# Finer TensorE steps, an earlier x load and new scheduling parameters in a two-part attention kernel

## The chip, the cores and the metric

The kernel runs on one core of one Trainium2 chip. The metric is device microseconds (us) of that core. Executions of one kernel differ here by several tenths of a per cent (11 runs of the kernel before took 1116.76 to 1122.92 us beside experiments 1 to 4), which is as large as some of the effects below. Where the text speaks of a time it is the median of several executions; where it speaks of a place in time, it is one profiled execution.

Names in the profile: PE is TensorE's matmuls and PEld its weight loads, DVE is VectorE, ACT is ScalarE, POOL is GpSimd, SP is SyncE (here it issues DMAs), and a trailing q is an engine's queue. "L970" is line 970 of the kernel's source. The change moves lines, so one group has another number before and after:

| work | before | after |
|---|---|---|
| exponentials | L970 | L1002 |
| scores | L941 | L973 |
| P times V | L1075 | L1109 |
| projections | L655 | L688 |
| output matmuls | L1162, L1210 | L1197, L1244 |

## The reference

Two attentions over different inputs, joined on the last axis. Both have 2048 rows, D = 1024, and 32 heads of 32.

```python
def _A_ref(x, wqkv, wo):                         # full softmax attention
    qkv = (x @ wqkv).reshape(B, S, 3, H, Dh)...  # q, k, v
    scores = einsum('bhqd,bhkd->bhqk', q, k) * Dh ** (-0.5)
    o = einsum('bhqk,bhkd->bhqd', softmax(scores), v)
    return o... @ wo

def _B_ref(x, wq, wk, wv, wo, beta):             # 4 segments of 512 rows, causal, with a memory
    for s in range(4):
        a_dot = softmax(qs @ ks^T * scale + mask) @ vs
        a_mem = (phi(qs) @ M) / (phi(qs) @ z + 1e-06)
        o = g * a_mem + (1 - g) * a_dot          # g = sigmoid(beta), one per head
        M, z = M + phi(ks)^T @ vs, z + sum(phi(ks))
    return o... @ wo

return concatenate([A, B], axis=-1)              # (1, 2048, 2048), bf16
```

## The kernel before

While it is built, the kernel runs a small scheduler of its own in Python. Processes (generators) ask for instructions with `do(engine, function, reads, writes, cost, priority)`. They wait for events, or acquire banks from pools. The scheduler has a clock and a table of costs, and each time an engine is free it takes the ready request with the lowest priority number. What comes out is a fixed order of instructions for every engine, with waits on semaphores in it. So a priority or a pool decides at build time what stands in front of what, and a misjudged cost shows up in a trace as an engine that waits.

```python
    def dispatch(self, eng, t):                       # [... cut ...]
        for rq in self.q[eng]:
            ready = ...                               # when everything it reads or overwrites is done
            p = rq.prio() if callable(rq.prio) else rq.prio
            if ready <= self.now + 1e-9:
                if best is None or (p, rq.seq) < best[0]:
                    best = ((p, rq.seq), rq)
        if best is None:
            if eng == "PE" and self.fill:
                rq = self.fill(soon)                  # nothing useful is ready: perhaps a filler
```

Scores have priority 0. A batch of scores is 8 matmuls (4 heads, 2 key tiles, 256 queries) into two pairs of PSUM banks. There are three such pairs. Each pair is then read by one exponential of 128x1024 on ScalarE, 1184 of them in all, and is free again when the exponential is done.

```python
            yield do("PE", lambda e: f(e, mms), r=keys, w=w, cost=N256, prio=0, mode=ROW)      # scores
        ...
            yield do("ACT", lambda e: e.activation(ap, self.ps[:, pr[0]:pr[1] + 1, :], ACTF.Exp, scale=sc),
                     r=[("ps", bk) for bk in pr], w=keys, cost=0.9035, prio=0)
            Q.give(self.pairs, [pr])
```

Everything else on TensorE accumulates in the two remaining "side" banks. A projection or output job is 8 steps of 4 matmuls, each 512 wide. A P-times-V unit takes a side bank, waits for exponentials one after the other, and keeps the bank until its last.

```python
    def job(self, due, mm, keys, out, okey, wkeys, ...):
        bank, = yield acq(self.side, 1, due)
        for i in range(last + 1):
            yield do("PE", lambda e, i=i: mm(e, i, bank), ..., cost=N512 * n / 512, prio=...)

    def pv_unit(self, u, steps, half):                # [... cut ...]
        OB, = yield acq(self.side, 1, -1000)
        for si, (k, parts) in enumerate(steps):
            yield ("ev", ("ex", u, k))                # the k-th exponentials of this unit
            ...
                yield do("PE", f, ..., cost=N256 * w / 256, prio=self.pvprio, mode=COL)   # 4 V matmuls, then 4 with ones
```

The filler gives TensorE work where it has little. If TensorE was under 65% busy in the scheduler's last 3.4 us, it adds matmuls of zeros to a bank in which an accumulation is under way (`self.under`):

```python
        if sum(c for _, c in Q.recent) > self.par["fil"] * 3.4:     # fil = 0.65
            return None
        bank = None
        for b in (OB, SB):
            if b in self.under:
                bank = b
        if bank is None:
            return None
        ...                                            # 4 matmuls of zeros, start=False, stop=False
```

The first x chunk (512 rows) is loaded in four pieces (XS 0 to 3) and transposed on TensorE. The other chunks come by DMA transposes that are held back until all four pieces have landed:

```python
                yield do("SP", lambda e, q0=q0, src=src: e.dma_start(self.xA[:, :, q0:q0 + 2 * P], src, transpose=True),
                         r=[("XS", 3), ("XS", 2), ("XS", 1), ("XS", 0)] if c == 1 and t == 0 else [], ...)
            self.Q.fire(("xA", c))
```

A flag is computed (were the softmax sums in range?), every engine reads it, and in the good case each engine branches over a fallback.

## Time and profile before

| | before |
|---|---|
| time, median of 4 runs (us) | 1119.68 (1118.54 to 1120.42) |
| span of the profiled run (us) | 1117.4 |
| ScalarE busy | 98% |
| TensorE busy | 94% |
| first exponential starts / ends (us) | 10.38 / 11.40 |
| last exponential ends (us), and from there to the end | 1103.64, 13.75 |

First the head of the page of the kernel before (busy us, share of the span, instructions), then from its table of groups the exponentials and the main scores (busy us, mean ns of one, then the idle time in front of them and what ended it):

```profile
span 1117.4 us, 50583 instructions
...
PE 1045.8 (94%) x23493; PEld 512.1 (46%) x23493; DVE 726.3 (65%) x1467; ACT 1091.2 (98%) x1191; POOL 134.8 (12%) x287
...
L970 ACT ACTIVATE PT<-ps 128x1024 bf16<-128x1024 f32 x1164 | 1068.4, 1202 | 2.6 <-PE ps L941 2.4
...
L941 PE MATMUL ps<-QA,KA 32*128 32x256 bf16 x4096 | 204.1, 273 | 34.3 <-ACT PT L970 25.0
```

Two things are to be read here. ScalarE is the limit: 1164 of the exponentials take 1068.4 us, 0.918 us each. And 1202 ns for one with 0.918 us of busy time means that each starts before the one ahead of it has ended. TensorE is 94% busy too, but its score groups wait for the exponentials (25.0 us), while the exponentials waited only 2.4 us for scores.

The chain of waits of the kernel before says the same in time order (start us, length us, what, how many). Long unbroken runs of exponentials carry most of the span:

```profile
48.88 1.07 issue
50.27 8.36 ACT PT L970 x9
58.70 74.26 ACT PT L970 x81
...
467.18 261.38 ACT PT L970 x285
728.57 373.24 ACT PT L970 x407
...
1104.25 0.87 PE ps L1075 x32
1105.12 2.59 PE ps L1162 x48
1108.36 4.16 PE ps L1162 x74
1112.54 0.58 ACT outsb L1168
```

373.24 us for 407 exponentials is 0.917 us each. The piece called "issue" is a stretch in which TensorE stood still although the profile shows nothing that it waited for. The last four lines are the tail: after the last exponential (1103.64) TensorE still has P times V and output matmuls to do.

The wait list of ScalarE, kernel before (us in total, times, longest):

```profile
ACT WoB L970 <- PE ps L941: 7.5, 2, 6.6
...
ACT OTA L970 <- PE ps L941: 2.6, 1, 2.6
...
ACT PT L970 <- PE ps L941: 2.4, 5, 1.0
```

6.6 us is the wait for the first scores. The 2.6 us is one wait near 21 us. The timeline of the kernel before shows where it comes from (start us, length us, engine, line, operation, count, idle time before and its releaser):

```profile
8.34 4.25 SPq L620 DMA_TRANSPOSE xA<-in_A_x_dram  x2
...
13.24 5.61 ACT L970 ACTIVATE WoB<-ps 128x1024 bf16<-128x1024 f32 x6 [0.93 <-PE ps L941]
...
16.70 4.35 PE L655 MATMUL ps<-xA,WA 128*32 128x512 bf16 x52
...
20.99 0.40 PE L941 MATMUL ps<-QA,KA 32*128 32x256 bf16 x8
...
21.43 5.61 ACT L970 ACTIVATE OTA<-ps 128x1024 bf16<-128x1024 f32 x6 [2.58 <-PE ps L941]
```

The transposes of the second x chunk are issued from 8.34 us on, when the fourth piece of the first chunk has landed, and their own data land at 13.0 and 15.9 us. The K projection of that chunk starts at 16.70, the scores follow at 20.99, and ScalarE, done at 18.85, waits until 21.43. The stretch view of the kernel before gives, for each stretch, length, busy time of PE, PEld, DVE, ACT and POOL, then the granted TensorE clock (PEclk), DMA share and GB/s:

```profile
12.70:16.10 3.40, 0.89 (x24) 0.27 (x16) 0.42 (x1) 2.85 (x4) 0.00 (x0) 1.00 1.24 197
16.10:19.50 3.40, 3.35 (x36) 1.22 (x40) 0.00 (x0) 2.75 (x3) 0.00 (x0) 0.50 1.62 204
```

After a stretch in which TensorE was 26% busy (0.89 of 3.40) comes one at half the clock, in which a 512-wide step took 0.427 us in place of 0.2155. In the traces of the whole programs here, the half-clock stretches that end before the work does last 3.413 us, or two or three times that, and within a trace they begin on one grid of 3.413 us. The kernel before has two of them, at 16.1 and at 285.7 us, each of 3.413 us; their starts are 269.65 us apart, 79 times 3.413. The first is part of the 2.6 us wait: the eight steps of that K projection took 3.11 us in place of 8 x 0.2155 = 1.72, so an estimate of 1.4 us of the wait is the clock's.

**Counting on ends.** Starts of exponentials are irregular; ends are not. From end to end there are 0.9167 us nearly everywhere, so time is lost for good only where a gap between ends is larger. I worked out from the traces the sum of what gaps of 0.925 us and more have above the mean of the other gaps. The profiled span is then an exact sum:

span = first end + 1183 x 0.9167 + losses + tail = 11.40 + 1084.4 + 7.84 + 13.75 = 1117.4 us.

The losses of the kernel before are 5.13 us before 60 us (1.03 at 12.3 us, 2.69 at 18.9, 0.25 at 28.9, 1.09 at 49.3 just after the "issue" pause, 0.07) and 2.70 us in all the rest.

### The profile page before, as it was taken

The numbers are of one execution on the slowest core, as the hardware profiler recorded it, in microseconds if no ns is written. First come the engines' busy times: TensorE is split into PE (matmuls) and PEld (weight loads), VectorE is DVE, ScalarE is ACT, GpSimd is POOL, SyncE is SP. The second block draws the span as 40 slices with busy tenths as digits, with TensorE's granted clock in tenths as the row PEclk, the third lists the DMA queues.
The fourth block names the chain that finished last, engine by engine and source line by source line (L and its number), as shares of the span: only waits on it lengthen the run. The fifth ranks groups of instructions, "written<-read, shape, count | busy, mean of one in ns | idle before, by whom it ended". The sixth has DMA issues, their size and how long they took to land.

```text
span 1117.4 us, 50583 instructions
## 1 busy us (share of the span) xinstructions
PE 1045.8 (94%) x23493; PEld 512.1 (46%) x23493; DVE 726.3 (65%) x1467; ACT 1091.2 (98%) x1191; POOL 134.8 (12%) x287
## 2 busy tenths in 40 slices
PE   8999999998999999999999899899999999999997
PEld 4444444444444444444444444444444444444443
DVE  2266666645674888889776877887666866753333
ACT  5999999999999999999999999999999999999996
POOL 1011111100201111211110301201111111110000
PEclk9999999999999999999999999999999999999999
DMA  9533331352111231253112223232222222201112
GB/s 186 101 85 103 64 78 33 68 88 45 41 41 31 64 74 40 46 96 65 45 40 60 45 59 51 50 85 52 50 48 56 48 42 46 86 17 36 36 40 71
DMA packets 213757, 67.31 MB, mean 60 GB/s; under 512 B 202786, under 2 KB 210978, under 8 KB 213538
## 3 DMA queue, kind: packets, MB, share of 16 engines
q1 hardware_dynamic: 212066, 63.07, 26.5%
q8 instruction: 186, 3.05, 1.2%
q10 hardware_dynamic: 1472, 0.92, 0.3%
q14 instruction: 33, 0.27, 0.1%
HBM read 36.70 MB, written 8.39 MB: 40 GB/s over the span
## 4 chain that ended last, share of the span: by engine, by line
ACT 88%; PE 7%; DVE 2%; DMA 1%; SPq 1%; issue 0%; DVEq 0%
ACT PT L970 87%; PE ps L655 3%; PE ps L1075 1%; PE ps L941 1%; PE ps L1162 1%; SPq L504 1%; DVE VT L661 0%; PE ps L548 0%; DMA PKt<-PH 0%; DMA VB<-VT 0%; ACT OTB L970 0%; ACT WoB L970 0%; DVE we L1006 0%; DVE ue L1002 0%; PE ps L590 0%
## 5 line engine op out<-in xcount | busy, mean ns | idle before, releaser
L970 ACT ACTIVATE PT<-ps 128x1024 bf16<-128x1024 f32 x1164 | 1068.4, 1202 | 2.6 <-PE ps L941 2.4
L1075 PE MATMUL ps<-PT,ones 128*32 128x256 bf16 (+1 forms) x4784 | 290.3, 270 | 0.0
L1075 PE MATMUL ps<-PT,VA 128*32 128x256 bf16 x4016 | 248.6, 275 | 11.2 <-ACT PT L970 7.5
L941 PE MATMUL ps<-QA,KA 32*128 32x256 bf16 x4096 | 204.1, 273 | 34.3 <-ACT PT L970 25.0
L655 PE MATMUL ps<-xB,WB 128*32 128x512 bf16 x3072 | 202.9, 381 | 2.0 <-DVE OD L1115 0.6
L655 PE MATMUL ps<-xA,WA 128*32 128x512 bf16 (+1 forms) x3136 | 202.3, 379 | 1.9 <-DVE xA L598 0.6
L979 POOL TENSOR_SCALAR_AFFINE_SELECT PT<-PT 128x256 bf16<-128x256 bf16 (+1 forms) x224 | 104.0, 469 | 793.8 <-ACT PT L970 788.3
L941 PEld LDWEIGHTS ps<-QA,KA 32*128 32x128 bf16 x4096 | 60.8, 92 | 206.6 <-ACT PT L970 193.6
L1075 PEld LDWEIGHTS ps<-PT,VA 128*32 128x32 bf16 x4016 | 106.7, 96 | 75.6 <-issue 27.1
L1075 PEld LDWEIGHTS ps<-PT,ones 128*32 128x32 bf16 x4784 | 128.0, 97 | 25.3 <-issue 0.3
L655 PEld LDWEIGHTS ps<-xA,WA 128*32 128x32 bf16 x3136 | 73.2, 96 | 76.6 <-issue 27.0
L1115 DVE COPY OD<-ps 128x512 f32<-128x512 f32 x127 | 86.6, 682 | 30.1 <-PE ps L1075 28.6
L655 PEld LDWEIGHTS ps<-xB,WB 128*32 128x32 bf16 x3072 | 71.2, 96 | 76.0 <-issue 31.0
L661 DVE CAST KQB<-ps 128x512 bf16<-128x512 f32 x64 | 44.0, 688 | 70.7 <-PE ps L655 70.5
L1168 DVE CAST outsb<-ps 128x512 bf16<-128x512 f32 x53 | 36.6, 691 | 77.9 <-PE ps L1162 77.6
L661 DVE CAST VT<-ps 128x512 bf16<-128x512 f32 x64 | 44.1, 688 | 61.6 <-PE ps L655 58.8
L1162 PE MATMUL ps<-WoB,OTB 128*32 128x512 bf16 x1024 | 68.2, 381 | 0.4
L1121 DVE STREAM_TRANSPOSE OD<-Rall 128x256 f32<-128x256 f32 x127 | 56.1, 442 | 3.3
L1118 DVE STREAM_TRANSPOSE Dt<-OD 128x256 f32<-128x256 f32 x127 | 55.5, 437 | 3.0
L1162 PE MATMUL ps<-xA,OTA 128*32 128x512 bf16 x832 | 53.6, 381 | 0.0
L1075 PE MATMUL ps<-PT,VB 128*32 128x256 bf16 (+1 forms) x768 | 45.2, 259 | 8.1 <-DVE OD L1115 3.1
L941 PE MATMUL ps<-KQB 32*128 32x128 bf16 (+3 forms) x512 | 43.3, 302 | 6.0 <-ACT PT L970 4.5
(95 smaller groups left out, 680.4 us busy)
## 6 DMA issues: line engine op xcount, KB each, us to landing
WB<-in_B_wk_dram SPq DMA_DIRECT2D x32, 256.0 KB, 2.9
WB<-in_B_wq_dram SPq DMA_DIRECT2D x32, 256.0 KB, 3.0
WB<-in_B_wv_dram SPq DMA_DIRECT2D x32, 256.0 KB, 3.2
out_dram<-outsb SPq DMA_DIRECT2D x63, 128.0 KB, 1.8
WA<-in_A_wqkv_dram SPq DMA_DIRECT2D x23, 256.0 KB, 3.2
WoB<-in_B_wo_dram SPq DMA_DIRECT2D x1, 2048.0 KB, 10.1
xA<-in_A_wo_dram SPq DMA_DIRECT2D x1, 2048.0 KB, 8.4
OTA<-in_A_x_dram SPq DMA_DIRECT2D x2, 256.0 KB, 5.0
```

The costliest lines, as they stand in the source:

```text
L504: yield do("SP", lambda e: e.dma_start(self.xB[:, :, :], src, transpose=True), w=["xB"], cost=5.2, prio=6, kb=1500)
L655: ins = e.matmul(self.ps[32 * c:32 * c + 32, bank, 0:n], W[:, i, 32 * c:32 * c + 32], x(i), start=(i == 0), stop=(i == NI - 1))
L661: return e.tensor_copy(dst, self.ps[:, bank, 0:n])
L941: ins = e.matmul(self.ps[:, bk, col:col + w], lhs(t, hs), rhs(q0, w, hs), start=True, stop=True)
L970: yield do("ACT", lambda e: e.activation(ap, self.ps[:, pr[0]:pr[1] + 1, :], ACTF.Exp, scale=sc), r=[("ps", bk) for bk in pr], w=keys, cos ...
L979: yield do("POOL", lambda e, m=m, n=n: e.affine_select(m, m, pattern=[[0, n], [1, P]], compare_op=ALU.is_ge, fill=0.0, base=0, channel_mul ...
L1075: ins = e.matmul(out, l, r, start=st, stop=sp)
L1115: yield do("DVE", lambda e: e.tensor_copy(OD[:, :], self.ps[:, OB, :]), r=[("ps", OB)], w=[("OD", x), ("Rb", x)], cost=dve(2 * QU), prio=0 ...
L1118: yield do("DVE", lambda e: e.transpose(Dt[:, :], Rb), r=[("Rb", x)], w=[("Dt", x)], cost=dve(QU), prio=self.par["fp"], hold=0.15)
L1121: yield do("DVE", lambda e: e.transpose(Rb.rearrange("p (a b) -> p a b", b=32), self.spread(Rc)), r=[("Rc", ui % 64)], w=[("Rb", x)], cost ...
L1162: ins = e.matmul(self.ps[32 * c:32 * c + 32, bank, :], lhs(j)[:, 32 * c:32 * c + 32], W(j), start=(j == 0), stop=(j == NG - 1))
L1168: return f(self.outsb[ob][:, :], self.ps[:, bank, :])
```

## The change

The intent: nothing should stand in front of the next scores. A whole projection step (0.216 us) or P-times-V step (0.22 us) that would run past the moment at which the next scores become ready is replaced by half a step. Work at the start is cut finer so that it can begin as soon as part of its data is there. Four parts:

1. **Splits.** Jobs get a half-width variant for each 512-wide step, used when the whole step would end later than the next scores' ready time plus 0.12 us and the half would not; a P-times-V step becomes two requests (V and ones).
2. **Start.** The first K chunks are projected in halves; projections wait for the 128-row pieces of x that they need; the x transposes are gated on two landed pieces in place of four.
3. **Filler.** It may also write into a side bank that is free.
4. **Parameters.** The memory matmuls are due earlier (mem -2 to -4), jobs may begin less far ahead (`ahead` 28 to 20), P times V has a higher priority (`pv` 24 to 10), output jobs are due earlier (`od` 4 to 2). And a P-times-V unit of attention A takes its bank only after the fourth of its exponential steps is done (`pvs`=3; below this is "the wait").

```diff
-    par = dict(... mem=-2, ... ahead=28, ... pv=24, ... od=4, ... pvw=3)
+    par = dict(... mem=-4, ... ahead=20, ... pv=10, ... od=2, ... pvw=3, pvs=3, slk=0.12, pat=0.0, kh=3)
@@ dispatch
+            if p == 0 and rq.mode == ROW and (sready is None or ready < sready):
+                sready = ready
+        part = False
+        if eng == "PE" and best is not None and best[0][0] > 0 and sready is not None:
+            rq = best[1]
+            late = sready + self.slack
+            c = 0.0 if rq.mode == self.mode else 0.1
+            if self.now + rq.cost + c > late:
+                if rq.half and self.now + rq.cost / 2 + c <= late:
+                    part = True
 [... cut: the second half is queued as a request of its own ...]
@@ filler
+        free = bank is None
+        if free:
+            for b in self.side.items:
+                if all(d.end + LAT <= now for d in Q.R.deps("PE", ["zero", "maskbd"], [("ps", b)])):
+                    bank = b
+                    break
 ...
-                ins = e.matmul(..., zero, src, start=False, stop=False)
+                ins = e.matmul(..., zero, src, start=free, stop=free)
@@ rest_x
-                         r=[("XS", 3), ("XS", 2), ("XS", 1), ("XS", 0)] if c == 1 and t == 0 else [], ...)
+                         r=[("XS", 1), ("XS", 0)] if c == 1 and t == 0 else [], ...)
+                for j in range(2):
+                    self.Q.fire(("xt", c, t + j))
@@ job
-            yield do("PE", lambda e, i=i: mm(e, i, bank), ...)
+            half = ((lambda e, ...: mm(e, i, bank, 0, h, st, False)), (lambda e, ...: mm(e, i, bank, h, n, False, sp)))
+            yield do("PE", fn, ..., half=half if n == 512 else None, ...)
@@ a_prep, group 0
+                two = w == "K" and c <= self.par["kh"]
+                todo += [(w, c, 4 * c, 4 * c + 2), (w, c, 4 * c + 2, 4 * c + 4)] if two else [(w, c, 4 * c, 4 * c + 4)]
@@ pv_unit
+        if u[0] == "A" and self.par["pvs"]:
+            yield ("ev", ("ex", u, self.par["pvs"]))
         OB, = yield acq(self.side, 1, -1000)
 ...
-                yield do("PE", f, ..., cost=N256 * w / 256, ...)
+                yield do("PE", lambda e, m=mms[:4]: f(e, m), ..., cost=N256 * w / 512, ...)
+                yield do("PE", lambda e, m=mms[4:]: f(e, m), ..., cost=N256 * w / 512, ...)
```

More of the change, by code (lines that the diff above doesn't have):

```diff
@@ L162 @@
 class Req:
-    __slots__ = ("eng", "fn", "r", "w", "cost", "prio", "mode", "tail", "proc", "seq", "order", "kb", "hold")
+    __slots__ = ("eng", "fn", "r", "w", "cost", "prio", "mode", "tail", "proc", "seq", "order", "kb", "hold", "half")
 class Pool:
@@ L193, in __init__ @@
         self.recent = []
+        self.slack, self.patience = 0.12, 0.0
         self.nfill = 0
@@ L285, in dispatch @@
             return
-        best, soon = None, None
+        best, soon, sready = None, None, None
         for rq in self.q[eng]:
@@ L304, in dispatch @@
                 soon = ready
+            if p == 0 and rq.mode == ROW and (sready is None or ready < sready):
[8 more added lines that the diff above has]
+                    part = True
+                elif sready - self.now < self.patience:
+                    best, soon = None, sready
         if best is None:
@@ L320, in dispatch @@
         assert all(k in self.R.lastw for k in rq.r), rq.r
+        if part:
+            rest = Req()
+            for k in Req.__slots__:
+                setattr(rest, k, getattr(rq, k))
+            rest.fn, rest.cost, rest.half = rq.half[1], rq.cost / 2, None
+            self.q[eng].append(rest)
+            rq.fn, rq.cost, rq.proc = rq.half[0], rq.cost / 2 + 0.003, None
         op = self.R.add("SP" if rq.kb else eng, rq.fn, rq.r, rq.w, rq.order, eng)
@@ L350, in run, with do @@
             raise RuntimeError(f"stuck processes: {self.nproc} " + str([k for k, v in self.events.items() if v is not True]))
-def do(eng, fn, r=(), w=(), cost=0.1, prio=5, mode=None, tail=None, order=None, kb=None, hold=0.0):
+def do(eng, fn, r=(), w=(), cost=0.1, prio=5, mode=None, tail=None, order=None, kb=None, hold=0.0, half=None):
     rq = Req()
+    rq.half = half
     rq.order, rq.kb, rq.hold = order, kb, hold
@@ L376 @@
 class Kernel:
-    par = dict(b=(16, 12, 9), mem=-2, memM=2, span=50, rate=0.58, ahead=28, sl=4, pv=24, ob=4, lead=6, b0=1, bpos=16, wob=40, mg=0.05, off=0, oks=(1,), sh=6, pd=4, o0=4, od=4, run=4, po=(1, 1), fp=2, fil=0.65, fs=0.15, ta=2, td=40, pvw=3)
+    par = dict(b=(16, 12, 9), mem=-4, memM=2, span=50, rate=0.58, ahead=20, sl=4, pv=10, ob=4, lead=6, b0=1, bpos=16, wob=40, mg=0.05, off=0, oks=(1,), sh=6, pd=4, o0=4, od=2, run=4, po=(1, 1), fp=2, fil=0.65, fs=0.15, ta=2, td=40, pvw=3, pvs=3, slk=0.12, pat=0.0, kh=3)
     def __init__(self, nc, A_x, A_wqkv, A_wo, B_x, B_wq, B_wk, B_wv, B_wo, B_beta, out):
@@ L571, in f @@
             for c in range(4):
-                ins = e.matmul(self.ps[32 * c:32 * c + 32, bank, 0:256], zero, src, start=False, stop=False)
+                ins = e.matmul(self.ps[32 * c:32 * c + 32, bank, 0:256], zero, src, start=free, stop=free)
             return ins
@@ L599, in first_x @@
         for t in range(4):
-            yield ("ev", ("x0t", t))
+            yield ("ev", ("xt", 0, t))
             if t % 2:
@@ L606, in one @@
         yield op
-        self.Q.fire(("x0t", t))
+        self.Q.fire(("xt", 0, t))
     def load_xs(self, t, via):
@@ L620, in rest_x @@
                 yield do("SP", lambda e, q0=q0, src=src: e.dma_start(self.xA[:, :, q0:q0 + 2 * P], src, transpose=True),
-                         r=[("XS", 3), ("XS", 2), ("XS", 1), ("XS", 0)] if c == 1 and t == 0 else [], w=[("xA", c, t), ("xA", c, t + 1)], cost=2.6, prio=1, kb=680)
+                         r=[("XS", 1), ("XS", 0)] if c == 1 and t == 0 else [], w=[("xA", c, t), ("xA", c, t + 1)], cost=2.6, prio=1, kb=680)
+                for j in range(2):
+                    self.Q.fire(("xt", c, t + j))
             self.Q.fire(("xA", c))
@@ L632, in job @@
                 yield ("ev", gate[1])
-            yield do("PE", lambda e, i=i: mm(e, i, bank), r=keys[i] + list(wkeys), w=[("ps", bank)], cost=N512 * n / 512,
+            h = n // 2
+            st, sp = i == 0, i == last
+            fn = lambda e, i=i, st=st, sp=sp: mm(e, i, bank, 0, n, st, sp)
+            half = ((lambda e, i=i, st=st: mm(e, i, bank, 0, h, st, False)), (lambda e, i=i, sp=sp: mm(e, i, bank, h, n, False, sp)))
+            yield do("PE", fn, r=keys[i] + list(wkeys), w=[("ps", bank)], cost=N512 * n / 512, half=half if n == 512 else None,
                      prio=(lambda: self.jprio(due)) if i == 0 else (lambda: min(self.jprio(due), self.par["run"])), mode=COL)
@@ L652, in proj, with mm @@
     def proj(self, due, W, wkey, x, xkeys, dst, dkeys, scale=None, n=512):
-        def mm(e, i, bank):
+        def mm(e, i, bank, lo, hi, st, sp):
             for c in range(4):
-                ins = e.matmul(self.ps[32 * c:32 * c + 32, bank, 0:n], W[:, i, 32 * c:32 * c + 32], x(i),
-                               start=(i == 0), stop=(i == NI - 1))
+                ins = e.matmul(self.ps[32 * c:32 * c + 32, bank, lo:hi], W[:, i, 32 * c:32 * c + 32], x(i)[:, lo:hi], start=st, stop=sp)
             return ins
@@ L686, in a_prep @@
         if g == 0:
-            todo[0:2] = [("K", 0, 0, 2), ("Q", 0, 0, 2), ("K", 0, 2, 4), ("Q", 0, 2, 4)]
+            todo = [("K", 0, 0, 2), ("Q", 0, 0, 2), ("K", 0, 2, 4), ("Q", 0, 2, 4)]
+            for w, c in order[2:]:
+                two = w == "K" and c <= self.par["kh"]
+                todo += [(w, c, 4 * c, 4 * c + 2), (w, c, 4 * c + 2, 4 * c + 4)] if two else [(w, c, 4 * c, 4 * c + 4)]
         if g == 0:
@@ L708, in a_stream @@
             yield ("ev", ("WA", k, g))
-            if t1 - t0 < 4:
-                for t in range(t0, t1):
-                    yield ("ev", ("x0t", t))
-            else:
-                yield ("ev", ("xA", c))
+            for t in range(t0, t1):
+                yield ("ev", ("xt", c, t % 4))
             d = due[(w, c)]
@@ L730, in a_stream @@
                     Q.fire((w + "A", g, i))
-            if c == 3 and g + 1 < NG:
+            if t1 == 16 and g + 1 < NG:
                 Q.spawn(self.load_WA(k, g + 1))
@@ L1071, in pv_unit, with f @@
                         mms.append((out, lhsT, rhs, first and not ones, last and ones))
-                def f(e, mms=mms):
+                def f(e, mms):
                     for out, l, r, st, sp in mms:
@@ L1076, in f @@
                     return ins
-                yield do("PE", f, r=sorted(pk, key=str) + vkeys + ["ones32"], w=[("ps", OB)], cost=N256 * w / 256,
-                         prio=self.pvprio, mode=COL)
+                rk = sorted(pk, key=str)
+                yield do("PE", lambda e, m=mms[:4]: f(e, m), r=rk + vkeys, w=[("ps", OB)], cost=N256 * w / 512, prio=self.pvprio, mode=COL)
+                yield do("PE", lambda e, m=mms[4:]: f(e, m), r=rk + ["ones32"], w=[("ps", OB)], cost=N256 * w / 512, prio=self.pvprio, mode=COL)
                 first = False
@@ L1158, in out_rows, with mm @@
         ob, = yield acq(self.outs, 1, due)
-        def mm(e, j, bank):
+        def mm(e, j, bank, lo, hi, st, sp):
             for c in range(4):
-                ins = e.matmul(self.ps[32 * c:32 * c + 32, bank, :], lhs(j)[:, 32 * c:32 * c + 32], W(j),
-                               start=(j == 0), stop=(j == NG - 1))
+                ins = e.matmul(self.ps[32 * c:32 * c + 32, bank, lo:hi], lhs(j)[:, 32 * c:32 * c + 32], W(j)[:, lo:hi], start=st, stop=sp)
             return ins
@@ L1206, in out_ahead, with mm @@
         lhs = lambda j: self.OTA[:, j, q0:q0 + P]
-        def mm(e, j, bank, only=False):
+        def mm(e, j, bank, lo, hi, st, sp):
             for c in range(4):
-                ins = e.matmul(self.ps[32 * c:32 * c + 32, bank, :], lhs(j)[:, 32 * c:32 * c + 32], self.WoA[:, j, ns],
-                               start=(j == 0 or only), stop=(j == NG - 2 or only))
+                ins = e.matmul(self.ps[32 * c:32 * c + 32, bank, lo:hi], lhs(j)[:, 32 * c:32 * c + 32], self.WoA[:, j, 512 * half + lo:512 * half + hi],
+                               start=st, stop=sp)
             return ins
@@ L1217, in out_ahead @@
         ob, = yield acq(self.outs, 1, d)
-        yield from self.job(-99, lambda e, j, bank: mm(e, NG - 1, bank, True), [[("OTA", NG - 1, qb // 2)]],
+        yield from self.job(-99, lambda e, j, *a: mm(e, NG - 1, *a), [[("OTA", NG - 1, qb // 2)]],
                             lambda e, bank, eng: e.tensor_tensor(self.outsb[ob][:, :], self.ps[:, bank, :], part, ALU.add),
@@ L1441, in main @@
         self.Q.fill = self.filler
+        Q.slack, Q.patience = self.par["slk"], self.par["pat"]
         self.slots = Pool([((0, 2 * i), (0, 2 * i + 1)) for i in range(RING // 2)])
```

## The prediction

> **What bounds it now.** ScalarE. The page has it busy for 98% of 1117.4 us, TensorE 94%. The chain of waits gives 88% to the exponentials (L970), in unbroken runs: 407 in 373.24 us, 285 in 261.38, 81 in 74.26. All are 0.917 us per exponential of 128x1024. [...] So 1184 exponentials take about 1085 us, which the change leaves alone.
>
> The rest: 10.4 us before the first exponential starts (timeline), waits between exponentials, and 13.75 us from the last exponential's end (1103.64) to the span's end.
>
> Between exponentials, starts are often 0.904 us apart, then one comes 50 to 130 ns "late" because scores waited behind a 0.22 us projection step. Over the run late starts sum to about 23 us. But ends come every 0.915 to 0.918 us through most of these: duration grows from 1.02 to 1.33 us as starts run ahead, and a late start only uses this lead up. Counted on ends, only 7.8 us are lost: 1.0 at 12.3 us, 2.7 at 18.9 (K of the second chunk is late: its x landed at 13.0 and 15.9, and its projection starts at 16.7), 0.25 at 28.9, 1.1 at 49.3 (TensorE pauses inside a score group, "issue"), and only about 2.8 after that.
>
> **What the change does.** By the order of instructions:
> 1. 161 projection or output steps (0.216 us) split in two; P-times-V steps (0.22) become two of 0.11. Same columns. The lead already hides late starts: worth 0 to 1 us.
> 2. K chunks of group 0 in halves; x transposes gated on two landings (4.5, 4.8 us) instead of four (8.3), so they can issue up to 3.5 us earlier. K's first half of chunk 1 is placed before the fourth score group. The 2.7 us gap goes, and 0 to 0.3 us of the first: 2.8 us.
> 3. Priorities (ahead, pv, mem, od) and 53 more filler groups (0.2 us each, in idle TensorE time): the steady part changes by -1 to +1 us. The 1.1 us pause depends on timing: half of it, 0.5 us.
> 4. Tail. After the last scores, output matmuls fall from 176 to 112 (64 x 54 ns = 3.4 us), P-times-V groups rise from 4 to 6 (+0.4). TensorE is full from 1104 to 1112.5 us, so nearly all is on the path: say 3.3 us.
>
> Sum: about 7 us. **1112.6 us, 80% range 1109.0 to 1117.0.** Faster by over 2% (below 1097.3): 0.01; within 2%: 0.98; slower: 0.01. Without any listed loss, and 3.7 us of tail, about 1108 remain.
>
> **What would show it.** Exponentials in long runs still 0.917 us each. ScalarE's 2.6 us wait for scores near 21 us gone; x chunk 1 landing near 10 to 13 us. First exponential unchanged at 10.4 us. Last exponential to end of span near 10.3 us. Fewer late starts, but almost the same total of late ends after 60 us.
>
> **What would make it wrong.** Earlier transposes slow the loads of x and of the weights, moving the first scores; new in-order stalls on TensorE; the freed score path shortening the 0.917 us itself, if TensorE set it (then several us more); the tail held by evictions and output DMAs instead of TensorE.

## The result, and the profile after

| | before | after |
|---|---|---|
| time, median of 4 runs (us) | 1119.68 | 1114.38 (1112.38 to 1116.19) |
| ratio after / before | | 0.9953, 95% interval 0.9932 to 0.9975 |
| profiled span (us) | 1117.385 | 1111.554 |
| first exponential ends | 11.40 | 11.39 |
| 1183 exponentials at 0.9167 | 1084.4 | 1084.4 |
| losses on ends, before 60 us | 5.13 | 1.93 |
| losses on ends, after 60 us | 2.70 | 2.71 |
| last exponential's end to the end | 13.75 | 11.13 |
| late starts after 60 us | 132, 14.5 us | 89, 9.0 us |

A ratio is the mean time of one kernel's fast runs over that of the other's in the same rounds, so it is not quite the ratio of the medians. A "late start" is one more than 0.930 us after the start before it; beside the count stands the sum of what they have above 0.904 us. In the profiled pair the saving is 5.8 us: 3.2 early, 2.6 in the tail, nothing between. The medians differ by 5.3.

The head of the page of the kernel after, and its exponentials:

```profile
span 1111.6 us, 52489 instructions
...
PE 1043.3 (94%) x24445; PEld 539.9 (49%) x24445; DVE 725.5 (65%) x1472; ACT 1089.7 (98%) x1189; POOL 136.8 (12%) x287
...
L1002 ACT ACTIVATE PT<-ps 128x1024 bf16<-128x1024 f32 x1164 | 1068.2, 1265 | 2.7 <-PE ps L973 2.5
```

The busy time of the exponentials is the same to 0.2 us. Only the mean length of one grew from 1202 to 1265 ns: they start earlier, because fewer of them start late, and end when they did.

The chain of waits of the kernel after. The pause ("issue") is still there; the runs of exponentials are longer, at the same 0.917 us (570.38 / 622); the tail's last piece of output matmuls is shorter:

```profile
46.80 1.16 issue
...
148.64 570.38 ACT PT L1002 x622
...
723.17 217.36 ACT PT L1002 x237
...
946.30 133.05 ACT PT L1002 x145
...
1104.23 1.57 PE ps L1197 x28
1105.81 0.57 ACT outsb L1202
```

ScalarE's wait list, kernel after: the entry of 2.6 us is gone.

```profile
ACT WoB L1002 <- PE ps L973: 7.3, 2, 6.6
...
ACT PT L1002 <- PE ps L973: 2.5, 6, 0.7
```

And the timeline of the kernel after, at the start:

```profile
5.30 6.39 SPq L647 DMA_TRANSPOSE xA<-in_A_x_dram  x2
...
12.96 5.69 ACT L1002 ACTIVATE WoB<-ps 128x1024 bf16<-128x1024 f32 x6 [0.66 <-PE ps L973]
...
14.76 1.27 PE L688 MATMUL ps<-xA,WA 128*32 128x256 bf16 x36
...
15.96 0.40 PE L973 MATMUL ps<-QA,KA 32*128 32x256 bf16 x8
...
18.51 7.61 ACT L1002 ACTIVATE OTA<-ps 128x1024 bf16<-128x1024 f32 x8
```

The first transpose is issued 3.0 us earlier, the first half of chunk 1 landed at 12.20 and the second at 13.78. The half projection starts at 14.76 and takes 1.27 us, and the exponential at 18.51 has no idle time before it. There is also no half-clock stretch in this trace before the work ends. All three traces with the old start (before, and experiments 3 and 4) have one at 15.8 to 16.8 us, and none of the ten with the new start has, so in the profiled runs the new start saved both the late data and the slow clock. Of the early losses there remain 0.76 us at 12.3, 0.08 and 0.14, and 0.62 and 0.23 just after the pause.

The tail in the timeline of the kernel after, its last rows:

```profile
1105.57 0.17 PE L1300 MATMUL ps<-badb,ones 128*32 128x1 bf16 x1
1105.80 0.58 ACT L1202 CAST outsb<-ps 128x512 bf16<-128x512 f32 x1 [0.71 <-PE ps L1197]
1105.83 0.15 DVE L1302 CAST flag<-ps 32x1 int32<-32x1 f32 x1 [0.41 <-PE ps L1197]
1106.41 0.36 ACTq L1204 DMA_DIRECT2D out_dram<-outsb  x1
```

and the rows for the same things before:

```profile
1109.10 0.14 DVE L1268 CAST flag<-ps 32x1 int32<-32x1 f32 x1 [1.00 <-PE ps L1162]
...
1112.54 0.58 ACT L1168 CAST outsb<-ps 128x512 bf16<-128x512 f32 x1 [1.14 <-PE ps L1162]
1113.15 0.36 ACTq L1170 DMA_DIRECT2D out_dram<-outsb  x1
```

TensorE's last output matmul ends 5.32 us after the last exponential, against 8.84 before: 3.5 us saved, where the count of matmuls in the prediction gave 3.4 less 0.4. But from there to the end of the span it now takes 5.8 us, against 4.9. Before, the flag was ready at 1109.2, in front of the last 64 output matmuls, and the last output landed 1.26 us before the end. After, the flag is the last thing computed, and the last output landed at 1108.28, 3.3 us before the end: the program is finishing something else. In the two traces, VectorE, ScalarE, GpSimd and SyncE need 2.6 to 3.6 us from their branch over the fallback to their next instruction (SyncE: branch at 1106.72, next at 1110.00; before, 1112.94 and 1116.23). TensorE's branch takes longer still: it is recorded from 1106.58 to 1111.19, 4.6 us (before, 1111.38 to 1115.67, 4.3 us). After the change TensorE is the last engine to reach the barrier at which all of them meet, at 1111.25, 0.3 us before the end. Before the change SyncE was the last; its branch stood behind its output DMAs. So the end after the change looks held by the flag and TensorE's branch, and not by output. This is read from the two traces; no run tests it.

### The profile page after: what moved, and what is told of

It is laid out like the page before. It is cut to its first block, busy times and chain, and to the rows that moved or that the text cites. A ratio compares the mean times of both kernels' runs of the same rounds, so it can differ in the third digit from the quotient of the medians.

```text
span 1111.6 us, 52489 instructions
## 1 busy us (share of the span) xinstructions
PE 1043.3 (94%) x24445; PEld 539.9 (49%) x24445; DVE 725.5 (65%) x1472; ACT 1089.7 (98%) x1189; POOL 136.8 (12%) x287
## 4 chain that ended last, share of the span: by engine, by line
ACT 90%; PE 6%; DVE 2%; DMA 1%; POOL 1%; issue 0%
ACT PT L1002 89%; PE ps L688 2%; PE ps L1109 2%; PE ps L1197 1%; PE ps L973 1%; DMA PKt<-PH 1%; ACT OTA L1002 1%; POOL PT L1011 0%; DMA OTA<-in_A_x_dram 0%; ACT OTB L1002 0%; DVE xA L625 0%; DVE VT L693 0%; PE ps L1244 0%; DVE PH L831 0%; DVE PH L1039 0%
## 5 line engine op out<-in xcount | busy, mean ns | idle before, releaser
L1002 ACT ACTIVATE PT<-ps 128x1024 bf16<-128x1024 f32 x1164 | 1068.2, 1265 | 2.7 <-PE ps L973 2.5
L1109 PE MATMUL ps<-PT,ones 128*32 128x256 bf16 (+1 forms) x4784 | 283.6, 270 | 1.2 <-issue 1.2
L1109 PE MATMUL ps<-PT,VA 128*32 128x256 bf16 x4016 | 241.3, 274 | 6.1 <-ACT PT L1002 5.0
L688 PE MATMUL ps<-xB,WB 128*32 128x512 bf16 (+1 forms) x3332 | 205.3, 364 | 2.4 <-DVE OD L1150 0.7
L1011 POOL TENSOR_SCALAR_AFFINE_SELECT PT<-PT 128x256 bf16<-128x256 bf16 (+1 forms) x224 | 106.5, 483 | 814.2 <-ACT PT L1002 808.9
L688 PE MATMUL ps<-xA,WA 128*32 128x512 bf16 (+1 forms) x3476 | 205.2, 356 | 1.3 <-DVE xA L625 0.6
L1109 PEld LDWEIGHTS ps<-PT,ones 128*32 128x32 bf16 x4784 | 128.0, 97 | 32.8 <-issue 16.5
L688 PEld LDWEIGHTS ps<-xA,WA 128*32 128x32 bf16 x3476 | 80.4, 96 | 78.6 <-issue 28.0
L688 PEld LDWEIGHTS ps<-xB,WB 128*32 128x32 bf16 x3332 | 77.3, 96 | 77.7 <-issue 31.3
L1197 PE MATMUL ps<-WoB,OTB 128*32 128x512 bf16 (+1 forms) x1100 | 68.2, 366 | 0.6 <-DVE OD L1150 0.6
L1197 PE MATMUL ps<-xA,OTA 128*32 128x512 bf16 (+1 forms) x888 | 53.4, 367 | 0.3 <-DVE KQB L693 0.3
```

The source lines that it names most:

```text
L688: ins = e.matmul(self.ps[32 * c:32 * c + 32, bank, lo:hi], W[:, i, 32 * c:32 * c + 32], x(i)[:, lo:hi], start=st, stop=sp)
L1011: yield do("POOL", lambda e, m=m, n=n: e.affine_select(m, m, pattern=[[0, n], [1, P]], compare_op=ALU.is_ge, fill=0.0, base=0, channel_mul ...
L1109: ins = e.matmul(out, l, r, start=st, stop=sp)
L1197: ins = e.matmul(self.ps[32 * c:32 * c + 32, bank, lo:hi], lhs(j)[:, 32 * c:32 * c + 32], W(j)[:, lo:hi], start=st, stop=sp)
```

## The experiments

Twelve kernels ran in three groups, each group on one chip beside runs of the kernel before. The theory after the result, in short: (i) ScalarE's end-to-end time is fixed at 0.917 us, so splits are worth nothing; (ii) the start gives 3 us; (iii) the new parameters and the filler give the tail and must go together. The rivals are told at each experiment.

### 1. Are the ends of exponentials real? (act_alone)

Duration grows from 1.02 us to 1.33 us along a run of exponentials while ends keep their 0.917 us. If ends in the trace are right (theory A), a late start costs nothing as long as there is lead. If ends are drawn wrongly and the engine's true pace is the 0.904 us between starts (rival B), every late start costs, and splits would be worth about 5 us. The edit puts a bench in place of the program. Its output is wrong, which doesn't matter for the time.

```diff
-            self.main()
+            self.bench()   # 60 plain exponentials of 128x1024 alone, 60 beside 480 groups of TensorE matmuls,
+                           # 60 beside 75 VectorE copies from PSUM, 60 of 128x512, 40 with f32 output
```

> Wrong result on purpose: only exponentials from PSUM to SBUF, in five stretches: 60 of 128x1024 alone, 60 beside TensorE matmuls, 60 beside VectorE copies out of PSUM, 60 of 128x512, 40 of 128x1024 with float32 output. Theory A (the 0.917 us between ends is ScalarE's own rate, which no order on TensorE can change): the ends are 0.917 us apart, within 0.004, in the first three stretches alike, and starts run ahead of ends until the duration stops growing near 1.33 us. Rival B (0.917 is a rate that TensorE or VectorE traffic slows, or that scores set): alone the ends come at 0.905 us or less, and beside traffic they are longer. No view on the 512 and float32 stretches beyond 0.917 minus about 0.43 for half the width.

Measured, 128x1024 to bf16 where nothing else is said:

| | start to start (us) | end to end (us) |
|---|---|---|
| alone | 0.9045 | 0.9170 |
| beside TensorE | 0.9045 | 0.9168 |
| beside VectorE | 0.9045 | 0.9168 |
| 128x512 | 0.4775 | 0.4901 |
| float32 output | 0.9042 | 0.9167 |

In the list of groups of this bench, and in its timeline where TensorE, which waits for the first 60, begins:

```profile
L416 ACT ACTIVATE PT<-ps 128x1024 bf16<-128x1024 f32 x180 | 165.4, 1380 | 110.4 <-PE ps L422 55.6 <-DVE OD L428 54.4 <-DVE OD L431 0.3
```

```profile
53.92 8.09 ACT L416 ACTIVATE PT<-ps 128x1024 bf16<-128x1024 f32 x8
...
62.06 2.32 PE L422 MATMUL ps<-maskbd,zero 128*32 128x256 bf16 x40 [56.89 <-ACT PT L416]
```

165.4 us for 180 is 0.919 each: the pace of the real kernel is ScalarE's own, with nothing beside it. The recorded end of the last of the first 60 is 62.01, and TensorE starts 0.05 us later; VectorE, after the next 60, 0.03 us after the end. An engine that depends on the exponential starts right after the recorded end, so the ends are real: A holds, B falls. One expectation of A missed: the duration does not stop at 1.33 us here but grows to the last of the 60 (1024 to 1761 ns). In the real kernel it stops there (longest 1.339 us before, 1.340 after) because the next scores wait for the bank that an exponential releases at its end: scores start 0.06 us after the end, and the next exponential on that pair 0.45 us after the scores.

From 512 to 1024 columns the time between ends grows by 0.4267 to 0.4269 us (0.9168 and 0.9170 less 0.4901), 0.833 to 0.834 ns for each of the 512 columns more. If the first 512 cost as much each, which was not measured, I estimate from these numbers that 63 ns of an exponential do not depend on its width.

### 2. The start alone (o_start)

The kernel after, without splits, with the old filler and the old parameters.

```diff
-    mem=-4 ahead=20 pv=10 od=2 pvs=3
+    mem=-2 ahead=28 pv=24 od=4 pvs=0
-        free = bank is None
+        free = False
-            ... half=half if n == 512 else None
+            ... half=None            # and P times V as one request again
```

> Before plus only the start of the change: K chunks of group 0 in halves, waits on single x pieces, x transposes gated on two loads. No step splitting, old priorities, old filler. Theory A (lost time counted on the ends of exponentials; the start is worth about 3.2 us): losses on ends before 60 us fall from 5.1 to between 1.2 and 2.2 us, the end of the last exponential moves 2.5 to 3.5 us earlier, the tail stays at 13.7 within 0.4; time 3 us (2 to 4) below before. Rival B (late starts are what the change repairs, as its intent says): the start is worth at most 1 to 1.5 us, as ScalarE catches up later.

Measured 1117.09 us against 1120.16 for the kernel before, ratio 0.9981 (0.9960 to 1.0001): 3.1 us. On ends, the early loss is 1.42 us (before 5.13), the tail 13.56, both as expected. The 2.7 us gap is gone, and no tail comes with it. The last exponential ended 2.24 us earlier, a little short of the expected 2.5, because in this execution the first one ended 0.53 us later and the mean pace was slower (0.9171 us, 0.5 us over the run). The interval of the ratio just reaches 1, so it is the ends, and not the times alone, that show the gain.

### 3. Splits alone (o_split)

The kernel before, with the splits and nothing else.

```diff
 the kernel after, with
+    mem=-2 ahead=28 pv=24 od=4 pvs=0; free = False
+    x transposes gated on XS 0 to 3 again, first K chunks whole again
```

> Before plus only the splitting of projection, output and P-times-V steps in halves with the rule that chooses them; old start, old priorities, old filler. Theory A: fewer late starts, but losses on ends unchanged within 1.5 us and tail unchanged (140 output matmuls after the last P-times-V, 136 in before); time within 1.5 us of before. Rival B: if a late start costs its excess, the 12 us of late starts after 50 us shrink by half or more and the time falls by 4 us or more.

Measured 1133.39 us, ratio 1.0128 (1.0101 to 1.0155): 13 us slower than before, where next to nothing was expected. The expectation failed. ScalarE's timeline in this kernel (L999 are its exponentials, L970 its scores) shows the largest piece:

```profile
841.50 4.97 ACT L999 ACTIVATE PT<-ps 128x1024 bf16<-128x1024 f32 x5
853.72 2.85 ACT L999 ACTIVATE PT<-ps 128x1024 bf16<-128x1024 f32 x3 [7.24 <-PE ps L970]
```

One wait of 7.24 us for scores. In the order of instructions the scheduler had put 8.1 us of TensorE work (worked out from its columns) between two score groups: a unit of attention B had its K and Q projected only just before its own scores, and everything else that was ready came along. The tail is 16.5 us. So splits do not only split: with shorter steps the scheduler makes other choices afterwards, and with the old parameters it runs into a late projection. In the order of the kernel before, the largest block after the first five score groups is 1.94 us; in that of the kernel after, none is above 1.75 us once the first scores have run.

### 4. Parameters alone (o_params)

The kernel before, with the new parameters including the wait, and nothing else.

```diff
 the kernel before, with
+    mem=-4 ahead=20 pv=10 od=2 pvs=3
```

> Before plus only the new priorities (mem, ahead, pv, od, and the wait for the fourth exponential of a unit before its P-times-V starts). Old start, whole steps, old filler. Theory A: the tail falls from 13.75 to about 11.1 us, as the order has 72 output matmuls after the last P-times-V in place of 136 (64 x 54 ns = 3.4 us, less what waits take back); losses on ends before 60 us stay at 5 us, later ones within 1.5 us of before; time 2 to 3.5 us below before. Rival B: the tail hangs on evictions and output DMAs, and shortens by less than 1 us.

Measured 1128.90 us, ratio 1.0094 (1.0067 to 1.0122): 8.7 us slower, where a gain was expected. The tail did become shorter (12.1 us, expected 11.1), but there is a loss of 5.1 us at 58 us, where two projections of xB stand back to back at half clock, and five half-clock stretches before the work ends (at 16.8, 54.3, 231.8, 696.1, 962.3 us; before had two). The granted clock was 0.983 to 0.989 in its runs.

So of four parts, two made the kernel slower alone, by 13 and 9 us, and yet the sum of all is 5 us faster. (The new filler was never run alone.) The next groups take the parts away from the other side.

### 5. The change again (after_again)

No edit; the kernel after, on the chip of the next three.

> The changed kernel unaltered, for comparison on this chip. As in its first trace: losses on the ends of exponentials near 2 us before 60 us and 2 to 4 us later, tail 11.1 us within 0.4; 4 to 6.5 us below before. Theory C (run-to-run scatter comes from 3.41 us stretches at half TensorE clock): a run whose granted clock is 0.001 lower takes about 1 us longer, in this kernel as in before.

Measured 1114.26 against 1120.65, ratio 0.9953 (0.9935 to 0.9972). The saving repeats. In its profile the tail is 11.10 us, losses 3.80 before 60 us and 1.75 after: in this execution there was a half-clock stretch at 49.3 us, just after the pause. So of the early saving only 1.3 us was left in this profile, where a loss near 2 us had been expected.

### 6. The change without the splits (u_split)

```diff
-            ... half=half if n == 512 else None
+            ... half=None
-                yield do("PE", ... m=mms[:4] ...)
-                yield do("PE", ... m=mms[4:] ...)
+                yield do("PE", ... m=mms ..., cost=N256 * w / 256, ...)
```

> The changed kernel with the splitting undone: whole projection, output and P-times-V steps; start, priorities and filler as changed. Its order has no new long block of TensorE work between score groups (longest 1.8 us by columns, at the 24th group) and the same 72 output matmuls after the last P-times-V. Theory A (splitting is worth nothing on the ends; the two slow runs were slow through long blocks in their orders): more late starts, losses on ends within 1.5 us of the changed kernel, tail within 0.5; time within 1.5 us of the changed kernel. Rival B: the splitting is what makes the new priorities work, and the time goes up by 3 us or more, as in the run with the priorities alone.

Measured 1114.46, ratio 0.9954 (0.9935 to 0.9972), against 1114.26 with splits on the same chip. The late starts are back: 129, with 13.4 us, as many as before the change (132, 14.5 us). And the medians are the same to 0.2 us, with intervals of about 2 us to either side. Losses on ends are 5.6 us in its profile (4.6 and 5.6 in the two of the kernel after), and the tail is 11.93 us, 0.8 more, where at most 0.5 had been expected. So late starts cost nothing that shows, and splits are worth less here than these runs can resolve, as theory (i) says.

### 7. The change with the old filler (u_fill)

```diff
-        free = bank is None
+        free = False
```

> The changed kernel with the filler limited to banks in use, as before. 61 filler groups in place of 122, and, as the schedule shifts, 140 output matmuls after the last P-times-V in place of 72; no long blocks. Theory A (the tail is bound by TensorE's output matmuls after the last P-times-V): tail 13.3 to 14.2 us in place of 11.1, so 2 to 3 us slower than the changed kernel. Rival (tail bound by evictions and DMAs): tail within 0.8 us of 11.1. Theory C adds: granted clock lower, 0.994 to 0.998, for 1 to 3 us more.

Measured 1118.15, ratio 0.9985 (0.9966 to 1.0003): 3.9 us are given back, by the filler alone. In its profile they are all in the tail: 15.37 us (expected 13.3 to 14.2), while losses on ends are 3.65 us in all, less than those of the kernel after (4.64). The filler occupies time in the scheduler's clock and so changes the order: after the last scores there are 164 output and 80 P-times-V matmuls, against 112 and 48 in the kernel after. The clocks are also lower, 0.992 to 0.996.

### 8. More filler (fil80)

If half-clock stretches make the scatter of the runs and the last losses, a filler that acts at 80% should gain 1 to 2 us.

```diff
-    fil=0.65
+    fil=0.8
```

> The changed kernel with filler whenever TensorE was busy for less than 80% of the last 3.4 us, in place of 65%: 184 filler groups in place of 122; tail order the same (72), no long blocks. Theory C (half-clock stretches follow a poorly filled 3.4 us): granted clock 0.999 to 1.000 in all runs, scatter under 1.5 us, median 1 to 2 us below the changed kernel. If filler does not govern the clock, or delays scores: no change or slower, and the scatter stays near 4 us.

Measured 1113.93, ratio 0.9949 (0.9931 to 0.9967): 0.3 us less than the kernel after, within the scatter. The runs still range over 3 us (1112.11 to 1115.16). Mostly a miss: the granted clocks were 0.997 to 0.999 (0.996 to 0.998 in the kernel after on this chip), where 0.999 to 1.000 in all runs had been expected, so more filler did not end the half-clock stretches.

### 9 to 11. Which parameter does what (p_no_mem, p_nopvs2, p_pvs)

These three start from the kernel of experiment 2 (new start, no splits, old filler) and add parameters. `mem` stays at -2 in all.

p_pvs adds the wait alone:

```diff
 o_start, with
+    pvs=3
```

> Before plus the start and that one line alone; pv, od, ahead and mem old, no splitting, old filler. The order has one block of 2.4 us near three quarters and 104 output matmuls after the last P-times-V. Theory A: losses before 60 us 1.5 to 4 us, one gap of 0.5 to 1.5 us for the block, tail between the two groups, 12 to 13 us; time 1115 to 1118.5 us, between the run with the start alone (1117.1) and the changed kernel.

p_nopvs2 adds the three priorities alone:

```diff
 o_start, with
+    ahead=20 pv=10 od=2
```

> The run without mem and splitting, less one line: P-times-V takes its bank without waiting for the unit's fourth exponential. The order now shows one block of 8.85 us of TensorE work between two score groups (near three quarters of the run) and 136 output matmuls after the last P-times-V. Theory A: one gap of 7 to 9 us between ends of exponentials near 845 us, a tail of 13.5 to 16 us, so 9 to 13 us slower than the run with the line, 1123 to 1128 us. If the order's blocks do not tell the time: within 3 us of it.

p_no_mem adds both:

```diff
 o_start, with
+    ahead=20 pv=10 od=2 pvs=3
```

> The changed kernel without any splitting, with the old filler and the old mem: what remains of the change is the start (K halves, gates) and four scheduling values (pv 10, od 2, ahead 20, and the wait of a unit's P-times-V for its fourth exponential). Its order has no long TensorE block between scores (longest 1.76 us) and 72 output matmuls after the last P-times-V. Theory A: it is as fast as the changed kernel, within 1.5 us (1113 to 1116 us), with losses on ends before 60 us of 1.5 to 4 us, later 1.5 to 4, tail 11 to 12 us, though its late starts are as many as in before. Rival B (the splitting carries part of the gain): slower by 2.5 us or more.

Together with the kernels above they make a ladder. Losses, tail and half-clock stretches before the work's end are of the profiled run, clocks of all runs:

| kernel | ratio to before | loss <60 us | loss >60 us | tail | stretches | clock |
|---|---|---|---|---|---|---|
| o_start | 0.9981 | 1.42 | 3.12 | 13.56 | 0 | .995 to .999 |
| + the wait (p_pvs) | 1.0034 | 5.56 | 10.01 | 12.03 | 6 | .985 to .989 |
| + priorities (p_nopvs2) | 1.0046 | 1.09 | 13.00 | 13.86 | 1 | .997 to .998 |
| + both (p_no_mem) | 0.9984 | 5.57 | 4.47 | 11.68 | 4 | .986 to .993 |
| + new filler, mem=-4 (u_split) | 0.9954 | 3.32 | 2.32 | 11.93 | 1 | .994 to .998 |
| + splits (after) | 0.9953 | 1.93 | 2.71 | 11.13 | 0 | .996 to 1.000 |

Medians: p_pvs 1124.40, p_nopvs2 1125.45, p_no_mem 1118.66, with 1120.07 for the kernel before on that chip. The expectation for p_nopvs2 held in its time, its gap (8.06 us) and its tail, but it is 6.8 us slower than p_no_mem, and not 9 to 13. Those for p_pvs and p_no_mem missed: both are slower than expected. By the terms put down for p_no_mem, rival B (the splits carry part of the gain) would hold; experiment 6, which has no splits either and is as fast as the kernel after, speaks against it. The timelines of p_nopvs2 show what priorities without the wait do. First ScalarE, then TensorE in the same place:

```profile
833.17 5.77 ACT L1002 ACTIVATE PT<-ps 128x1024 bf16<-128x1024 f32 x6
846.89 2.85 ACT L1002 ACTIVATE PT<-ps 128x1024 bf16<-128x1024 f32 x3 [7.95 <-PE ps L973]
```

```profile
839.44 1.47 PE L688 MATMUL ps<-xA,WA 128*32 128x512 bf16 x24
840.73 1.90 PE L688 MATMUL ps<-xB,WB 128*32 128x512 bf16 x32
842.46 0.60 PE L688 MATMUL ps<-xA,WA 128*32 128x512 bf16 x8
843.52 1.91 PE L688 MATMUL ps<-xB,WB 128*32 128x512 bf16 x32 [0.46 <-DVE KQB L693]
845.25 1.27 PE L688 MATMUL ps<-xA,WA 128*32 128x512 bf16 x20
846.45 0.39 PE L973 MATMUL ps<-KQB 32*128 32x512 bf16 x4
```

Both projections of xB, which are the K and Q of the unit whose scores come at 846.45, run in those 7 us, one after the other. This is the block of experiment 3 at the same place in the program. In the order of no kernel with the wait is any block near there longer than 2.8 us, and p_no_mem, which differs from p_nopvs2 by the wait alone, has no such gap: that the wait removes the block is shown. A likely reason, which is argued and not tested by itself: a P-times-V unit that takes one of the two side banks before its exponentials are done keeps it from a projection that is soon due; with the wait the projection gets the bank earlier.

p_pvs shows the price of the wait. P times V now holds a bank for a shorter time, and the old filler can write only into a bank with an accumulation under way, so it finds a place less often: the wait takes the filler groups from 69 (o_start) to 42 (p_pvs), and from 95 (p_nopvs2) to 54 (p_no_mem). In u_split, where the new filler may use a free bank, there are 128. The profiled runs of the three kernels with the wait, the old filler and no splits (o_params, p_pvs, p_no_mem) have 4 to 6 half-clock stretches, and their runs clocks of 0.983 to 0.993. The only steps from p_no_mem to u_split are the new filler and `mem`: the clock rises to 0.994 to 0.998, the profiled losses fall from 10.0 to 5.6 us, and the ratio from 0.9984 to 0.9954. The two were not separated here, so filler and `mem` share those 3 to 4 us. Experiment 7 takes back the filler alone, with splits, and loses 3.9 us; but its profile has only two half-clock stretches and loses them in the tail, so it is not shown that the filler acts through the clock.

### 12. The pause (bpos12)

In five traces (before, after, after again, more filler, and this one) TensorE starts nothing for 1.0 to 1.8 us once, between 41 and 50 us, in the middle of a group. In all of them it does so after the same place in its instruction stream (after 1729, 1730 or 1985 TensorE instructions of the trace, weight loads included, which is 193 or 194 above a multiple of 256), and near the end of a packet of 16 KB on the DMA queue that the page lists as `q8 instruction`: the last start before the pause lies between 0.3 us before that packet has come in and 0.5 us after. Except in the last kernel, the DMA transposes of attention B's x end during the pause. Experiments 2, 3, 4 and 7 have a pause at the same place too, of 0.7 to 1.7 us. To learn whether the load or the place in the program decides, the B load is made earlier.

```diff
-    bpos=16
+    bpos=12
```

> The changed kernel with the loads of the second half's x and weights started four score groups (7.3 us) earlier. Order without long blocks, same tail. Question: TensorE pauses 1.0 to 1.7 us near 46.3 us with nothing to wait for, and goes on 0.2 to 0.4 us after this x load lands (47.1 to 47.6 us). Theory D (the load holds TensorE's instructions up): the load lands near 40 us, and the pause ends within 0.5 us of its landing, or there is none. Rival (the pause belongs to that place in the program): it stays near 46 us. Time within 1.5 us of the changed kernel either way.

Measured 1113.50, ratio 0.9944 (0.9932 to 0.9957). The pause moved with the load, from about 46.5 to 41.93 us, and became shorter, 0.96 us; it again lies at such a place in the program. But it ended 2.1 us before the load had landed, so neither theory as put down fits, and the cause stays open. A third, that TensorE waits for its next instructions, fits the place and the packet; no run tests it. The profiled run was the fastest of all (1109.2 us); the median is 0.8 us below that of the kernel after on another chip, which is within the scatter of either. It is no proven improvement.

### The scatter

In the 11 runs of the kernel before of the first group, the time goes with the mean granted clock: the correlation is -0.89, with 1.09 us for each 0.001 of clock; in the 11 of the second and of the third group it is -0.77 and -0.82, with 0.79 and 0.69 us. Runs at 0.999 took 1116.8 and 1117.9 us, runs at 0.995 took 1120.8, 1122.2 and 1122.9. So much of the scatter of 3 to 6 us between executions of one kernel goes with the half-clock stretches; that they cause it is argued and not tested. In the second group the mean clock was 0.9965 before and 0.9973 after, so by these slopes I estimate that 0.6 to 0.9 of the 5.4 us between the means is clock. For what starts a stretch the traces give a rule at the ends and none between. I laid the 13 traces of whole programs on their grids and took the stretches at full clock, from 9 us on. All 19 in which TensorE was less than half busy (25 to just under 50%) were followed by half clock, and none of the over 4000 that were more than 62% busy. Between, 7 of 33 were: in the kernel before one that was 61% busy (282.3 to 285.7 us, 2.06 of 3.40 us), in the kernel after none of three that were 51 to 58% busy.

## Why the prediction was right, point by point

Predicted were 1112.6 us (1109 to 1117) and 98% for "within 2%". Measured were 1114.38 us and a ratio of 0.9953. The saving was 5.3 us in the medians where 7.1 were predicted (5.8 in the profiled pair).

- **ScalarE sets the pace, at 0.917 us, and the change leaves it alone:** right. 0.917 in the long runs of both kernels, busy time 1068.4 and 1068.2 us. Experiment 1 shows that it is ScalarE's own pace: 0.917 with nothing beside it.
- **Splits are worth 0 to 1 us:** right within what the runs resolve, 0.2 us (experiment 6, intervals of about 2 us). The reason given, that a late start only uses up lead, is shown twice: by the ends in experiment 1 and by 129 late starts that cost nothing in experiment 6. The kernel's author aimed at these late starts, and the profile's 25 us of score groups that wait for exponentials invite the same aim.
- **The start gives 2.8 us, and half the pause another 0.5:** right in the sum, 3.2 us in the profiled pair; 3.1 in the medians for the start alone. The sum owes something to luck: in the second profile the early saving was 1.3 us, with a half-clock stretch after the pause. The first landing fits (12.20 us for "10 to 13"), the second was late (13.78), the first exponential started at 10.37 for 10.38, and the wait near 21 us is gone. The pause is still there; it cost 0.85 us in place of 1.09.
- **The steady part changes by -1 to +1 us:** right in the sum (2.70 and 2.71 us), but too lightly argued, and so in part by luck. I treated the parameters and the filler as small and separable. They are not: alone, splits cost 13 us and parameters 9, the wait alone 6 to 7 and the priorities alone 7 to 8 on top of the new start. They cancel because one repairs what the other breaks: the wait clears the late projection (shown by one edit, p_nopvs2 to p_no_mem), and the new filler gives back what the wait loses (3.9 us in experiment 7; whether through the clock or through the order is open).
- **The tail gives 3.3 us:** the mis-sized term. It gave 2.6 (13.75 to 11.13, and 11.10 in the second profile). TensorE's part shrank by 3.5 us, a little more than counted (3.4 less 0.4, which the prediction rounded up to 3.3). But "TensorE is full from 1104 to 1112.5 us, so nearly all is on the path" overlooked that the flag, computed before the last 64 output matmuls in the kernel before, becomes the last thing of all; flag and branch (4.6 us on TensorE) then hold the end, and the part after TensorE's last matmul grew from 4.9 to 5.8 us. The list of what could go wrong named evictions and output DMAs, not the branch. That the branch holds the end is read from traces and not tested; an earlier flag would test it.
- **The rest of the difference** is 0.5 us for the splits, which were put into the sum at half their range, and 0.5 us between the profiled pair (5.8) and the medians (5.3): two of the four runs after had a clock of 0.996, while the profiled one had 1.000. The last is an attribution by the correlation above, not a test.

## What to carry to other kernels

When one engine is saturated, measure its losses on ends, not on starts: irregular starts that leave the end-to-end time alone cost nothing that showed here, and removing them gained nothing that showed (experiment 6: 129 late starts with whole steps, and 0.2 us between the medians). A change to a list scheduler cannot be costed part by part from its diff, because each part reorders the whole program; look at the order it makes for long blocks of other work between two groups of the critical kind, and for stretches of 3.4 us in which TensorE is left less than half busy (all 19 here were followed by half clock). And when a tail is shortened, ask what will be last afterwards, down to the flag and the branch.
